# Retention and a mixture of experts on one core: a state read spread over four array quarters, empty rows written one per pass, fill branches on two engines

## The chip, the cores and the metric

The kernel runs on one core of one Trainium2 chip. Its five engines are TensorE (PE in the profile; PEld is its weight load), VectorE (DVE), ScalarE (ACT), GpSimd (POOL) and SyncE (SP); each takes its instructions from a queue of its own, in order. The metric is the time of one execution on the device in microseconds (us), as the median of several runs.

## The reference

Inputs are q, k and v of 4 sequences, 8 heads, 768 tokens and 64 columns, two gates of 512 x 8 and, for each of 8 experts, w1 (512 x 1024) and w2 (1024 x 512). Cut to what matters:

```python
for t in range(S):                       # attention: a decaying state for each head
    state = gamma * state + k[t] outer v[t]
    y[t] = scale * q[t] @ state
x = y as rows of tokens (3072 x 512)
e_idx = argmax(x @ w_gate); gate_w = probability of e_idx; eom = sigmoid(x @ w_output_gate)
for e in range(E):                       # each token goes to one expert
    out[mask] = gate_w * eom[e] * (relu(x[mask] @ w1[e]) @ w2[e])
```

## The kernel before, in words

**Attention.** A sequence has six chunks of 128 tokens, taken in pairs: `j` counts 12 pairs, `NJ` = 3 to a sequence, and `c` is the chunk in a pair. Eight heads stand in four groups `g` of two halves `hh` (partitions 0 to 63 and 64 to 127). For a pair, `scores` (L349) multiplies k and q of each chunk, and VectorE masks the result into `ams[c]` (L359). `inter` (L367) reads the state: a matmul of 64 rows by 64 columns for each head, from `sd[j, c]` into the PSUM banks `py[0]` and `py[1]`, one bank for a chunk. For the second chunk the halves of the output are exchanged (`half[hh ^ c]`), so that the two chunks' matmuls lie on all four 64 x 64 quarters of the array. In the first pair of a sequence (j % NJ == 0) the first chunk has no state to read and is skipped; the second chunk's matmuls then lie on two quarters. `attend` (L376) adds the masked scores times v, bank by bank; `weigh` (L384) multiplies a bank by the decay `gq` on VectorE and writes `yts`. `state` (L390) updates the state. `turn_k` (L324, L328) and `turn_q` (L342, L346) transpose the next pair's k and q on PE and copy them out. For the pair before, `logits` (L407), `route1`, `exps`, `gates`, `counts` and `places` find each token's expert and row, `tokens` (L508) transposes y back, `rows` (L515, L518) copies it scaled into `row` on ScalarE, one copy for the first chunk and two for the second, whose halves are exchanged, and `scatter` (L532) writes its rows by an indirect DMA of GpSimd into `srt`, a table in HBM sorted by expert with 448 slots to each. `prep_q` (L298) and `prep_v` (L290) rearrange q and scale v. Before j = 1, `more_gq` (L282) builds `gq` chunk by chunk.

**Branches.** Where an expert has few tokens, slots have to be filled with empty rows. `fill` (L543) does this on GpSimd and VectorE under a condition read into a register: `late` (L734) in iteration j = 10, behind `inter(10)`, and `n_low` (L831) behind the last attention work. The register is loaded, and the branch taken, on all five engines. In the profiled execution nothing is filled.

**Experts.** The expert with the most tokens after a third of the work is started early: `run_head` works off its first 224 slots as matmuls between the last attention steps (L622, L643). Then eight passes follow, each with eight stages `s` of 128 hidden columns: `stage1` (L899) is 12 matmuls into `h`, `relu` (L903, L904) splits it into two parts, and `stage2` (L917) of the stage two before is 12 matmuls into `a`. Pass 0 is the rest of the first expert, 224 slots wide; passes 1 to 7 are 436 to 364 wide, by the number of tokens. `load_x` (L853) loads a pass's rows from `srt`, a pass ahead; `turn_x` and `low_x` (L872 to L883) transpose and split them into `xh` and `xw`. `load_weights` (L142, L146) brings the weights, `split_weights` (L159 to L165) splits them on ScalarE and VectorE. `emit_head` and `emit` (`send`, L177) write finished rows to the output by indirect DMAs of GpSimd.

**Empty rows.** Slots of an expert from 320 up to its end that hold no token are written with empty rows by `pad` (L187), one indirect DMA for each expert. One is issued in `head_load`; `new_pad` issues the others: three behind ReLU steps of `run_head` (`hd["relu", 5]` to `hd["relu", 7]`), and four in pass 0, each behind a `stage2` (`done`). `load_x(e)` waits for write `e`. A write is declared independent of the row loads in `x0`, which holds those of pass 0 alone. On GpSimd's queue the writes of pass 0 stand among the outputs of `emit_head`.

Of the kernel before, what the change touches and what calls it, by code (L numbers as in the profile page):

```python
# [15 lines left out]
AF = mybir.ActivationFunctionType  # L16
ALU = mybir.AluOpType
# [9 lines left out]
SEG = 130  # L27
ROW = 4 * SEG
NOID = float(1 << 20)


@with_exitstack
def retention_moe_kernel(
# [14 lines left out]
    nc = tc.nc  # L48
    P = 128
# [152 lines left out]
    with tc.manual_schedule(engines=None), ExitStack() as actx:  # L202
# [76 lines left out]
                nc.gpsimd.tensor_copy(gqn[h, 1], gqn[half[1 - n], 0])  # L279

        def more_gq(c, engine):
            engine.tensor_tensor(out=gq[:, c], in0=gqn[:, c % 2].rearrange("p g (t r) -> p g r t", r=2),  # L282
                                 in1=gc[:, c % 2, c, :].unsqueeze(2).unsqueeze(3).broadcast_to([P, NG, 2, 64]), op=ALU.mult)

        def prep_v(j, engine, parts=1):
            c0, src = 2 * (j % NJ), vn.pop(j)
# [77 lines left out]
        def open_y():  # L364
            rt["py"] = [ps_1.tile([P, 512], F32, name="py", tag=f"y{c}") for c in range(2)]

        def inter(j):  # L367
            for g in range(NG):
                for c in range(2):
                    if j % NJ == 0 and c == 0:  # L370
                        continue
                    for hh in range(2):
                        nc.tensor.matmul(rt["py"][c][half[hh ^ c], g * P:(g + 1) * P], sd[j, c][half[hh], g],  # L373
                                         qt[j][half[hh], g, c], start=(g == 0), stop=False, skip_group_check=True)

        def attend(j, c):  # L376
            py = rt["py"][c]
            for g in range(NG):
                for hh in range(2):
                    mm = nc.tensor.matmul(py[half[hh ^ c], g * P:(g + 1) * P], vs[j][:, c, 2 * g + hh], ams[c][:, hh, g],  # L380
                                     start=(j % NJ == 0 and c == 0 and g == 0), stop=True, skip_group_check=True)
            return mm.ins

        def weigh(j, c):  # L384
            if c == 0:
                yts[j] = ap.tile([P, 2, NG, P], F32, name="yt", tag="yt", bufs=2)
            nc.vector.tensor_tensor(out=yts[j][:, c].rearrange("p g t -> p (g t)"), in0=rt["py"][c],
                                    in1=gq[:, 2 * (j % NJ) + c].rearrange("p g r t -> p (g r t)"), op=ALU.mult)

        def state(j, c):  # L390
            if j % NJ == 0 and c == 0:
# [10 lines left out]
        def logits(j):  # L402
            misc = rt["misc"] = ps_1.tile([P, 512], F32, name="misc", tag="misc" if j + 1 < NPR else "st")
            for i in range(2):
                for t in range(4):
                    c, g = t // 2, 2 * (t % 2) + i
                    nc.tensor.matmul(misc[32 * t:32 * t + 32, 0:P], wg[:, c, g], yts[j][:, c, g], start=(i == 0), stop=(i == 1),  # L407
                                     tile_position=(0, 32 * t))
            lt = sm.tile([P, P], F32, name="lt", tag="lt")
            nc.scalar.copy(lt, misc[:, 0:P])  # L410
            rt["lt"] = lt
# [99 lines left out]
        def rows(j):  # L511
            px = rt.pop(("px", j))
            gate = rt.pop(("g", j))
            row = rt["row", j]
            nc.scalar.activation(row[:, 0, :, 0:P].rearrange("p a (dc j) -> p dc a j", j=32),  # L515
                                 px[:, 0].rearrange("p (dc a j) -> p dc a j", a=4, j=32), AF.Copy, scale=gate[:, 0:1])
            for x in range(2):
                nc.scalar.activation(row[:, 1, 2 - 2 * x:4 - 2 * x, 0:P].rearrange("p a (dc j) -> p dc a j", j=32),  # L518
                                     px[:, 1].rearrange("p (dc x a j) -> p x dc a j", x=2, a=2, j=32)[:, x],
                                     AF.Copy, scale=gate[:, 1:2])  # L520

        def labels(j):
# [175 lines left out]
        prep_q(1, nc.vector)  # L698
        state(0, 0)
        attend(0, 0)  # L700
        weigh(0, 0)
        more_gq(1, nc.vector)
        inter(0)
        turn_q(1, True)
        state(0, 1)
        turn_k(1, True)
        attend(0, 1)
        weigh(0, 1)
        swap_gates()
        last_consts()  # L710
# [3 lines left out]
        for j in range(1, NPR - 1):  # L714
            if j + 2 < NPR:
                load_pair(j + 2)
            if j - 1 == PICK + 1:
                read_pick()
            if j in w_at:
                load_weights(w_at[j])  # L720
            if j - 2 == EARLY:
                scatter(j - 2, 0)
                scatter(j - 2, 1)
            prep_q(j + 1, nc.gpsimd, [rt["done"]] if j >= 2 else ())
            prep_v(j + 1, nc.gpsimd)
            if j >= 2 and j - 2 != EARLY:
                scatter(j - 2, 0)
            open_y()
            scores(j, (lambda: state(1, 0)) if j == 1 else None)
            if j - 1 in w_at:  # L730
                cast_weights(w_at[j - 1])
            inter(j)
            if j == EARLY + 2:
                n_late = nc.values_load(late[0:1, 0:1], min_val=0, max_val=1)  # L734
                with tc.If(n_late > 0):
                    fill(base0, cnt0, 0, HEAD, sm)
                head_load()
                load_weights(4)
            logits(j - 1)
            turn_k(j + 1)  # L740
            turn_l(j - 1)
            route1(j - 1)
            exps(j - 1)
            attend(j, 0)
            weigh(j, 0)
            if j % NJ < NJ - 1:
                state(j, 1)
            turn_q(j + 1)
            gates(j - 1)
            for c in {1: (3, 4), 2: (5,)}.get(j, ()):  # L750
                more_gq(c, nc.vector)
            if j - 1 in w_at:
                low_weights(w_at[j - 1])
            if j - 2 == PICK:
                choose()
            tokens(j - 1)
            labels(j - 1)
            rows(j - 1)
            counts(j - 1)
            if j >= 2 and j - 2 != EARLY:  # L760
                scatter(j - 2, 1)
            places(j - 1)
            if j - 1 == PICK:
                sort8(cnts, io8, pick)
            if j - 1 == EARLY:
                judge()
            attend(j, 1)
            weigh(j, 1)
            state(j + 1, 0)
# [58 lines left out]
        cast_weights(6)  # L828
        run_head(12)
        low_weights(6)  # L830
        n_few = nc.values_load(n_low[0:1, 0:1], min_val=0, max_val=E)  # L831
        with tc.If(n_few > 0):
            for e in range(E):
                fill(float(e * SLOTS), cnts[:, e:e + 1], FILL - P, FILL, sm)
            n_few = nc.values_load(n_low[0:1, 1:2], min_val=0, max_val=E)
            with tc.If(n_few > 0):
                for e in range(E):
                    fill(float(e * SLOTS), cnts[:, e:e + 1], 0, FILL - P, sm)

    with tc.manual_schedule(engines=None), ExitStack() as mctx:  # L840
# [7 lines left out]
        def load_x(e):  # L848
            r0, n = PASS[e]
            nb = math.ceil(n / 32)  # L850
            t = mp.tile([P, NB, SEG], F32, name="xl", tag="xl")
            for a in range(4):
                ld = nc.sync.dma_start(  # L853
                    t[32 * a:32 * a + 32, 0:nb],
                    srt[ds(r0, 32 * nb), a * SEG:(a + 1) * SEG].rearrange("(n i) x -> i n x", i=32))
                if e == 0:
                    behind(ld, sent)
                    x0.append(ld.ins)
                else:
                    behind(ld, pads[e:e + 1])  # L860
                    for o in pads[:e] + pads[e + 1:]:
                        tc.declare_no_dep(ld.ins, o, reason="other experts' rows")
            xr[e] = t

        def turn_x(e, dc):
# [103 lines left out]
            nc.vector.tensor_scalar(out=t, in0=m, scalar1=0.25, scalar2=None, op0=ALU.mult)  # L969
            return t  # L970

        x0 = []
        pads = list(hd["pad"])

        def new_pad(after):
            r = len(pads)
            o = pad(padr[:, r - 1:r])
            behind(o, [after])
            for ld in x0:
                tc.declare_no_dep(o.ins, ld, reason="other experts' rows")  # L980
            pads.append(o.ins)

# [24 lines left out]
        nc.vector.tensor_scalar(out=padr, in0=fj, scalar1=slot, scalar2=None, op0=ALU.add)  # L1007
        new_pad(hd["relu", 5])
        run_head(24)
        new_pad(hd["relu", 6])  # L1010
        run_head(12)
        turn_x(0, 0)
        turn_x(0, 1)
# [28 lines left out]
        for s in range(NS + 2):  # L1042
# [9 lines left out]
                relu = stage1(s)  # L1052
            if s >= 2:
                done = stage2(s - 2)
                if s - 2 < NF and len(pads) < E:
                    new_pad(done)
                if f == 1:
                    copy_out(s - 2)
            if e == 0:
# [9 lines left out]
                        split_weights(n)  # L1069
            if s == NS - NF + 3:  # L1070
                idl = prep_idl(idm)
            if e == 0:
                if f < HEAD // 32:
                    behind(emit_head(f), [relu])
            elif s < NS and f >= 1:
                for n in range(2 * f - 2, min(math.ceil(PASS[e - 1][1] / 32), 2 * f)):
                    behind(emit(e - 1, n), [done if n % 2 else relu])
# [130 lines left out]
```

## Time and profile before

| what | value |
|---|---|
| three timed runs, us | 430.78, 431.31 (median), 432.47 |
| the profiled execution, us | 432.42 |
| its span in the profile, us | 430.65 |
| PE busy | 413.7 us, 96% |
| VectorE, ScalarE, GpSimd busy | 264.4, 179.3, 190.2 us |
| DMA | 74.06 MB, mean 172 GB/s |

The span runs from the first instruction of the program to the last; the execution's own time has some 1.8 us more. A timeline or chain row reads: start and duration in us, engine, line, operation, output<-inputs, number of instructions merged, and in brackets the idle time of the engine ahead of it with what ended it. "issue" there stands for time in which the engine waited for nothing that the profile shows. A row of stretches reads: window, its length, then for each engine the busy time and the number of its instructions, the granted clock of TensorE as a share of full speed, the DMA engines' busy share and what they moved. Attention runs up to about 124 us, the head of the first expert up to 148 us, the passes up to 420 us.

### The profile page before, as it was taken

What the parts mean: (1) busy time and instruction counts of PE and PEld (TensorE: products, weight loads), DVE (VectorE), ACT (ScalarE), POOL (GpSimd) and SP (SyncE); (2) the same over time, 40 slices, a digit from 0 to 9 for tenths busy, and PEclk for the clock granted to TensorE, in tenths of its full rate; (3) what the DMA queues carried; (4) which work ended last, traced back from release to release, by engine and by line L of the source; (5) the groups of instructions that cost most, each with busy time, mean ns of one, the idle gap of its engine ahead of it and who ended that gap; (6) DMA issues with size and microseconds to landing.
All of it is one profiled execution on the core that took longest, in us unless ns stands there. A gap on an engine that the chain in (4) does not pass through costs nothing.

```text
span 430.7 us, 10299 instructions
## 1 busy us (share of the span) xinstructions
PE 413.7 (96%) x3700; PEld 392.0 (91%) x3700; DVE 264.4 (61%) x703; ACT 179.3 (42%) x395; POOL 190.2 (44%) x257
## 2 busy tenths in 40 slices
PE   8999999999999998999999999999999999999990
PEld 4888999999879997899999999999999999999990
DVE  2888778778778765766466556655646656754120
ACT  2244565646436233635335334443434443542120
POOL 6558666676624217060045426405515524523512
PEclk9999999999999999999999999999999999999995
DMA  9999999995562398494475395485558458420102
GB/s 192 208 225 255 258 268 248 275 269 176 144 223 102 74 250 272 146 270 153 135 172 173 122 198 171 137 188 167 177 151 206 137 176 197 159 59 19 44 7 74
DMA packets 126566, 74.06 MB, mean 172 GB/s; under 512 B 56686, under 2 KB 114930, under 8 KB 126504
## 3 DMA queue, kind: packets, MB, share of 16 engines
q1 hardware_dynamic: 119568, 59.30, 55.1%
q0 software_dynamic: 5728, 13.93, 9.3%
q8 instruction: 31, 0.51, 0.5%
q14 instruction: 31, 0.25, 0.2%
q10 hardware_dynamic: 1208, 0.06, 0.2%
HBM read 59.35 MB, written 15.23 MB: 173 GB/s over the span
## 4 chain that ended last, share of the span: by engine, by line
PE 80%; issue 9%; DMA 3%; POOL 3%; DVE 2%; SPq 1%; ACT 1%; POOLq 0%; DVEq 0%; ACTq 0%
PE h L899 26%; PE a L917 26%; PE w L356 5%; PE py L380 5%; PE py L373 3%; POOL out_dram L177 3%; PE w L324 3%; PE w L342 2%; PE w L508 2%; PE st L396 2%; PE misc L407 2%; PE h L622 2%; DMA kn<-in_k_dram 1%; DMA srt<-row,posi 1%; PE w L643 1%
## 5 line engine op out<-in xcount | busy, mean ns | idle before, releaser
L177 POOL DMA_INDIRECT out_dram<-ot,idi x84 | 91.0, 1083 | 147.2 <-ACT whi L160 79.0
L899 PE MATMUL h<-xh,whi 128*128 128x224 f32 (+7 forms) x256 | 85.6, 334 | 1.1 <-issue 1.1
L899 PE MATMUL h<-xw,whi 128*128 128x224 f32 (+7 forms) x256 | 85.9, 335 | 0.6 <-issue 0.4
L899 PE MATMUL h<-xh,wlo 128*128 128x224 f32 (+7 forms) x256 | 85.4, 334 | 0.9 <-issue 0.9
L917 PE MATMUL a<-hh,whi 128*128 128x224 f32 (+7 forms) x256 | 85.8, 335 | 0.4 <-issue 0.3
L917 PE MATMUL a<-hl,whi 128*128 128x224 f32 (+7 forms) x256 | 85.8, 335 | 0.1
L917 PE MATMUL a<-hh,wlo 128*128 128x224 f32 (+7 forms) x256 | 85.7, 335 | 0.0
L904 DVE SCALAR_TENSOR_TENSOR hl<-h,hh 128x224 fp32r<-128x224 f32 (+7 forms) x64 | 35.0, 548 | 61.9 <-ACT hh L903 54.0
L903 ACT ACTIVATE hh<-h 128x224 fp32r<-128x224 f32 (+7 forms) x64 | 31.0, 484 | 82.1 <-PE h L899 74.7
L164 DVE TENSOR_TENSOR wlo<-raw,whi 128x512 fp32r<-128x512 f32 x64 | 43.9, 686 | 29.3 <-ACT whi L159 25.7
L159 ACT CAST whi<-raw 128x512 fp32r<-128x512 f32 x64 | 39.6, 619 | 37.7 <-PE a L917 33.4
L899 PEld LDWEIGHTS h<-xw,whi 128*128 128x128 f32 x256 | 48.2, 188 | 2.4 <-issue 1.3
L899 PEld LDWEIGHTS h<-xh,whi 128*128 128x128 f32 x256 | 48.2, 188 | 2.0 <-issue 1.6
L917 PEld LDWEIGHTS a<-hh,whi 128*128 128x128 f32 x256 | 48.2, 188 | 1.3 <-issue 0.9
L899 PEld LDWEIGHTS h<-xh,wlo 128*128 128x128 f32 x256 | 48.2, 188 | 0.9 <-issue 0.5
L917 PEld LDWEIGHTS a<-hl,whi 128*128 128x128 f32 x256 | 48.2, 188 | 0.6 <-DVE hl L904 0.2
L917 PEld LDWEIGHTS a<-hh,wlo 128*128 128x128 f32 x256 | 48.2, 188 | 0.4
L165 DVE TENSOR_TENSOR wlo<-raw,whi 128x512 fp32r<-128x512 f32 x64 | 43.8, 685 | 0.0
L160 ACT CAST whi<-raw 128x512 fp32r<-128x512 f32 x64 | 39.6, 618 | 0.1
L877 ACT CAST xh<-xt 128x416 fp32r<-128x416 f32 (+3 forms) x32 | 16.3, 513 | 40.4 <-DVE xt L876 29.8
L359 DVE TENSOR_TENSOR am<-w,mask 128x1024 f32<-128x1024 f32 x24 | 28.4, 1219 | 5.9 <-PE w L356 4.5
L532 POOL DMA_INDIRECT srt<-row,posi x24 | 24.7, 1030 | 11.0 <-issue 2.9
(183 smaller groups left out, 606.0 us busy)
## 6 DMA issues: line engine op xcount, KB each, us to landing
raw<-in_moe_w_dram SPq DMA_DIRECT2D x128, 256.0 KB
qn<-in_q_dram SPq DMA_DIRECT2D x12, 512.0 KB
kn<-in_k_dram SPq DMA_DIRECT2D x24, 256.0 KB
vn<-in_v_dram SPq DMA_DIRECT2D x24, 256.0 KB
xl<-srt SPq DMA_DIRECT2D x12, 211.2 KB
xl<-srt SPq DMA_DIRECT2D x12, 195.0 KB
out_dram<-ot,idi POOLq DMA_INDIRECT x84
xl<-srt SPq DMA_DIRECT2D x8, 113.8 KB
```

Of the source, the lines that this page charges most:

```text
L159: nc.scalar.copy(hi[:, 0], raw[:, 0])
L160: nc.scalar.copy(perm(hi), r2)
L164: nc.vector.tensor_sub(lo[:, 0], raw[:, 0], hi[:, 0].bitcast(F32))
L165: nc.vector.tensor_sub(perm(lo), r2, perm(hi).bitcast(F32))
L177: st = nc.gpsimd.indirect_dma_start(out=dst, out_offset=bass.IndirectOffsetOnAxis(ap=idx, axis=0), in_=src, in_offset=None, bounds_check=n ...
L356: nc.tensor.matmul(w[:, hh, g * P:(g + 1) * P], kt[j][half[hh], c, g], qt[j][half[hh], g, c], start=True, stop=True)
L359: nc.vector.tensor_tensor(out=a.rearrange("p b g t -> p (b g) t"), in0=w.rearrange("p b (g t) -> p (b g) t", g=NG), in1=mask.rearrange("p ...
L532: st = nc.gpsimd.indirect_dma_start(out=srt, out_offset=bass.IndirectOffsetOnAxis(ap=posi[:, c:c + 1], axis=0), in_=row[:, c].rearrange("p ...
L899: nc.tensor.matmul(ps[:, 0:C], l[:, 0, w], r[:, dc, 0:C], start=(n == 0), stop=(n == 3 * NDC - 1))
L903: relu = nc.scalar.activation(hh, ps[:, 0:C], AF.Relu)
L904: nc.vector.scalar_tensor_tensor(out=hl, in0=ps[:, 0:C], scalar=0.0, in1=hh.bitcast(F32), op0=ALU.max, op1=ALU.subtract)
L917: mm = nc.tensor.matmul(accs[d][:, 0:C], l[:, 1, w], r, start=(f == 0 and n == 0), stop=(f == NF - 1 and n == 2))
```

## The change

In the first pair of a sequence, `place` gives each chunk and group a bank, a place in it and whether its halves are exchanged: each bank then holds two groups of either chunk, and the second chunk's groups 2 and 3 aren't exchanged. `inter` goes through the groups in the order 0, 2, 1, 3; `attend` and `weigh` take a bank at a time, so that both chunks' masked scores are needed for the first bank (for j = 0 `attend` stays by chunk, and `weigh(0, 0)` moves behind `attend(0, 1)`). `more_gq(1)`, the gates in `logits` and the copies in `rows` follow the places; `rows` has four copies instead of three in these pairs. The register loads and branches at L734, L831 and L835 are made for GpSimd and VectorE alone. `new_pad` behind `hd["relu", 6]` and the four in pass 0 go; one stands at the first stage of each of the passes 1 to 5, behind that stage's ReLU. The writes are declared independent of all passes' row loads.

```diff
 NOID = float(1 << 20)
+FILLERS = (mybir.EngineType.Pool, mybir.EngineType.DVE)
...
         def more_gq(c, engine):
-            engine.tensor_tensor(out=gq[:, c], in0=gqn[:, c % 2].rearrange("p g (t r) -> p g r t", r=2),
-                                 in1=gc[:, c % 2, c, :].unsqueeze(2).unsqueeze(3).broadcast_to([P, NG, 2, 64]), op=ALU.mult)
+            for g, x in ((slice(0, 2), 1), (slice(2, 4), 0)) if c == 1 else ((slice(0, NG), c % 2),):
+                engine.tensor_tensor(out=gq[:, c, g], in0=gqn[:, x, g].rearrange("p g (t r) -> p g r t", r=2),
+                                     in1=gc[:, x, c, g].unsqueeze(2).unsqueeze(3).broadcast_to([P, g.stop - g.start, 2, 64]),
+                                     op=ALU.mult)
...
+        def mixed(j):
+            return j % NJ == 0
+
+        def place(j, c, g):
+
+            if not mixed(j):
+                return c, g, c
+            return (c ^ g // 2, 2 * c + g % 2, c ^ c * (g // 2))
+
         def inter(j):
-            for g in range(NG):
-                for c in range(2):
-                    if j % NJ == 0 and c == 0:
-                        continue
-                    for hh in range(2):
-                        nc.tensor.matmul(rt["py"][c][half[hh ^ c], g * P:(g + 1) * P], sd[j, c][half[hh], g],
-                                         qt[j][half[hh], g, c], start=(g == 0), stop=False, skip_group_check=True)
-
-        def attend(j, c):
-            py = rt["py"][c]
-            for g in range(NG):
+            todo = [(g, c) for g in range(NG) for c in range(2)]
+            if mixed(j):
+                todo = [(g, 1) for g in (0, 2, 1, 3)]
+            for g, c in todo:
+                b, n, x = place(j, c, g)
                 for hh in range(2):
-                    mm = nc.tensor.matmul(py[half[hh ^ c], g * P:(g + 1) * P], vs[j][:, c, 2 * g + hh], ams[c][:, hh, g],
-                                     start=(j % NJ == 0 and c == 0 and g == 0), stop=True, skip_group_check=True)
+                    nc.tensor.matmul(rt["py"][b][half[hh ^ x], n * P:(n + 1) * P], sd[j, c][half[hh], g],
+                                     qt[j][half[hh], g, c], start=(j > 0 and g in ((0, 2) if mixed(j) else (0,))), stop=False,
+                                     skip_group_check=True)
+
+        def attend(j, i):
+            todo = [(c, g) for c in range(2) for g in range(NG) if (place(j, c, g)[0] if j and mixed(j) else c) == i]
+            for c, g in todo:
+                b, n, x = place(j, c, g)
+                for hh in range(2):
+                    mm = nc.tensor.matmul(rt["py"][b][half[hh ^ x], n * P:(n + 1) * P], vs[j][:, c, 2 * g + hh], ams[c][:, hh, g],
+                                          start=(j == 0 and c == 0 and g % 2 == 0), stop=True, skip_group_check=True)
             return mm.ins
...
-        def weigh(j, c):
-            if c == 0:
+        def weigh(j, i):
+            if i == 0:
                 yts[j] = ap.tile([P, 2, NG, P], F32, name="yt", tag="yt", bufs=2)
-            nc.vector.tensor_tensor(out=yts[j][:, c].rearrange("p g t -> p (g t)"), in0=rt["py"][c],
-                                    in1=gq[:, 2 * (j % NJ) + c].rearrange("p g r t -> p (g r t)"), op=ALU.mult)
+            c = 2 * (j % NJ)
+            out = yts[j].rearrange("p c (a g) t -> p (c a) (g t)", a=2)
+            by = gq[:, c:c + 2].rearrange("p c (a g) r t -> p (c a) (g r t)", a=2)
+            w = (slice(0, 4, 3) if i == 0 else slice(1, 3)) if mixed(j) else slice(2 * i, 2 * i + 2)
+            nc.vector.tensor_tensor(out=out[:, w], in0=rt["py"][i].rearrange("p (a x) -> p a x", a=2), in1=by[:, w], op=ALU.mult)
...
                     c, g = t // 2, 2 * (t % 2) + i
-                    nc.tensor.matmul(misc[32 * t:32 * t + 32, 0:P], wg[:, c, g], yts[j][:, c, g], start=(i == 0), stop=(i == 1),
+                    nc.tensor.matmul(misc[32 * t:32 * t + 32, 0:P], wg[:, place(j, c, g)[2], g], yts[j][:, c, g], start=(i == 0), stop=(i == 1),
                                      tile_position=(0, 32 * t))
...
                                  px[:, 0].rearrange("p (dc a j) -> p dc a j", a=4, j=32), AF.Copy, scale=gate[:, 0:1])
+            n = 2 if mixed(j) else NG
             for x in range(2):
-                nc.scalar.activation(row[:, 1, 2 - 2 * x:4 - 2 * x, 0:P].rearrange("p a (dc j) -> p dc a j", j=32),
-                                     px[:, 1].rearrange("p (dc x a j) -> p x dc a j", x=2, a=2, j=32)[:, x],
+                nc.scalar.activation(row[:, 1, 2 - 2 * x:4 - 2 * x, 0:P].rearrange("p a (dc j) -> p dc a j", j=32)[:, 0:n],
+                                     px[:, 1].rearrange("p (dc x a j) -> p x dc a j", x=2, a=2, j=32)[:, x, 0:n],
+                                     AF.Copy, scale=gate[:, 1:2])
+            if n < NG:
+                nc.scalar.activation(row[:, 1, :, 0:P].rearrange("p a (dc j) -> p dc a j", j=32)[:, n:],
+                                     px[:, 1].rearrange("p (dc a j) -> p dc a j", a=4, j=32)[:, n:],
                                      AF.Copy, scale=gate[:, 1:2])
...
         attend(0, 0)
-        weigh(0, 0)
         more_gq(1, nc.vector)
...
         attend(0, 1)
+        weigh(0, 0)
         weigh(0, 1)
...
             if j == EARLY + 2:
-                n_late = nc.values_load(late[0:1, 0:1], min_val=0, max_val=1)
+                n_late = nc.values_load(late[0:1, 0:1], engines=FILLERS, min_val=0, max_val=1)
                 with tc.If(n_late > 0):
...
         low_weights(6)
-        n_few = nc.values_load(n_low[0:1, 0:1], min_val=0, max_val=E)
+        n_few = nc.values_load(n_low[0:1, 0:1], engines=FILLERS, min_val=0, max_val=E)
         with tc.If(n_few > 0):
...
                 fill(float(e * SLOTS), cnts[:, e:e + 1], FILL - P, FILL, sm)
-            n_few = nc.values_load(n_low[0:1, 1:2], min_val=0, max_val=E)
+            n_few = nc.values_load(n_low[0:1, 1:2], engines=FILLERS, min_val=0, max_val=E)
             with tc.If(n_few > 0):
...
                     behind(ld, sent)
-                    x0.append(ld.ins)
                 else:
...
                         tc.declare_no_dep(ld.ins, o, reason="other experts' rows")
+                xloads.append(ld.ins)
             xr[e] = t
...
-        x0 = []
+        xloads = []
         pads = list(hd["pad"])
...
             behind(o, [after])
-            for ld in x0:
+            for ld in xloads:
                 tc.declare_no_dep(o.ins, ld, reason="other experts' rows")
...
         run_head(24)
-        new_pad(hd["relu", 6])
         run_head(12)
...
                 done = stage2(s - 2)
-                if s - 2 < NF and len(pads) < E:
-                    new_pad(done)
                 if f == 1:
...
                 idl = prep_idl(idm)
+            if e > 0 and f == 0 and len(pads) < E:
+                new_pad(relu)
             if e == 0:
```

## Rows read from the trace of the kernel before

**Rows 1.** The page, part 1: engine, busy us (share of the span), instructions.

```profile
PE 413.7 (96%) x3700; PEld 392.0 (91%) x3700; DVE 264.4 (61%) x703; ACT 179.3 (42%) x395; POOL 190.2 (44%) x257
```

**Rows 2.** Stretches: PE, PEld, DVE, ACT, POOL busy (instructions), clock, DMA share, GB/s.

```profile
38.60:48.30 9.70, 9.70 (x162) 8.87 (x161) 7.38 (x38) 5.36 (x15) 6.36 (x11) 1.00 1.07 276
...
136.00:140.00 4.00, 4.00 (x38) 4.00 (x37) 3.23 (x12) 2.78 (x6) 1.28 (x2) 1.00 0.35 135
...
152.00:168.00 16.00, 15.95 (x143) 15.76 (x142) 10.10 (x28) 7.03 (x15) 6.76 (x7) 1.00 1.06 283
168.00:176.00 8.00, 5.26 (x28) 3.98 (x28) 2.37 (x5) 1.65 (x4) 4.11 (x5) 1.00 0.28 104
...
200.00:379.00 179.00, 179.00 (x986) 178.02 (x985) 108.10 (x191) 76.24 (x145) 71.00 (x65) 1.00 0.60 166
```

**Rows 3.** The chain that ended last: `inter` of j = 1 and j = 3.

```profile
21.03 1.03 PE py L373 x32
...
40.59 1.02 PE py L373 x16
```

**Rows 4.** The timeline of j = 3: the masks and the first `attend`.

```profile
39.95 2.36 DVE L359 TENSOR_TENSOR am<-w,mask 128x1024 f32<-128x1024 f32 x2
...
43.24 0.99 PE L380 MATMUL py<-am,vs 128*64 128x128 f32 x14
```

**Rows 5.** The timeline of j = 0 and 1.

```profile
13.64 0.76 DVE L298 COPY qr<-qn 128x512 f32<-128x512 f32 x2
14.21 1.23 PE L342 MATMUL w<-ident,qr 128*128 128x128 f32 x8
14.31 0.69 DVE L387 TENSOR_TENSOR yt<-py,gq 128x512 f32<-128x512 f32 x1
...
23.80 0.23 DVE L422 TENSOR_REDUCE lg<-misc 128x32 f32<-128x64 f32 x1 [1.50 <-PE misc L415]
...
28.44 0.69 ACT L515 ACTIVATE row<-w,gate 128x512 f32<-128x512 f32 x1 [1.11 <-DVE gate L463]
...
29.03 0.82 ACT L518 ACTIVATE row<-w,gate 128x256 f32<-128x256 f32 x2
```

**Rows 6.** Line L518: count, ns min/median/max, first and last start; who waited (us, times).

```profile
L518 ACT ACTIVATE row<-w,gate x24: 463/477/487, 29.0 to 134.0; 128x256 f32<-128x256 f32 x24
...
  PEld w L356: 0.3, 1
```

**Rows 7.** Lines L734 and L831, PE's own register loads, columns as in rows 6.

```profile
L734 PEldq TENSOR_LOAD <-late x1: 486/486/486, 108.7 to 108.7; - x1
...
L831 PEldq TENSOR_LOAD <-n_low x1: 312/312/312, 137.9 to 137.9; - x1
```

**Rows 8.** The timeline of PE: `inter(10)`.

```profile
107.30 1.09 PE L373 MATMUL py<-qt,sd 64*64 64x128 f32 x25
...
109.44 0.42 PE L373 MATMUL py<-qt,sd 64*64 64x128 f32 x2 [0.30 <-issue]
```

**Rows 9.** The timeline of pass 0: pass 1's rows, empty rows, outputs.

```profile
161.15 0.18 DVE L872 CAST idi<-xl 128x14 int32<-128x14 f32 x1 [1.38 <-DMA xl<-srt]
...
161.98 0.98 POOL L187 DMA_INDIRECT srt<-zrow,padr  x1 [7.67 <-PE h L899]
...
172.35 0.98 POOL L177 DMA_INDIRECT out_dram<-ot,idx  x1 [0.30 <-issue]
```

**Rows 10.** The chain at the end of pass 0: groups of 12 matmuls.

```profile
166.98 1.34 PE a L917 x12
...
176.07 2.37 PE h L899 x12
```

**Rows 11.** The timeline of the same stretch.

```profile
169.80 0.63 DVE L883 TENSOR_TENSOR xw<-xt,xh 128x448 fp32r<-128x448 f32 x1 [0.63 <-issue]
...
171.95 0.19 PEld L899 LDWEIGHTS h<-xh,whi 128*128 128x128 f32 x1 [0.84 <-issue]
...
174.92 0.36 ACT L903 ACTIVATE hh<-h 128x224 fp32r<-128x224 f32 x1 [5.15 <-PE h L899]
```

## Prediction before the result was known

> **What bounds the kernel now.** I read the page first: its busy shares name the engine that is hardly ever idle, TensorE (PE), with 413.7 us of a span of 430.7 [rows 1]. The table of stretches comes next, because a share over the whole span hides stages. PE has no idle time in an attention iteration (9.70 of 9.70 us) and none from 200 to 379 us (179.00 of 179.00), with the granted clock full; but from 168 to 176 us it works 5.26 us of 8.00 [rows 2]. So there are two ways to shorten this kernel: give PE less to do, or close that hole. The timeline and the chain then show what each edit touches. The profiled execution took 432.42 us (span 430.65, 1.77 us around it); the median of the three timed runs is 431.31. I make the sum against 432.42 and carry the difference, 1.11 us, over to the median.
>
> **The state read on four quarters.** In the first pair of each sequence (j = 0, 3, 6, 9) `inter` has only the second chunk to read, and all its matmuls use two of the four 64 x 64 quarters. Its 16 records take 1.02 us; in the other pairs 32 records on four quarters take 1.03 us [rows 3]. So 16 records on four quarters should need 0.51 us, and 0.51 us is saved per first pair. In j = 3, 6 and 9 PE waits for nothing, so I count 3 x 0.51 = 1.53 us. What could now be late: `attend(j, 0)` newly needs the masked scores of both chunks. In j = 3 VectorE finishes the second mask at 39.95 + 2.36 = 42.31 and `attend` starts at 43.24, so after a gain of 0.51 there are 0.42 us left [rows 4]. Were that cover gone, the cost would be the shortfall, at most 0.51 per pair. The weighing keeps one instruction per bank; that it now writes two pieces I cost at nothing, since VectorE waits 1.50 us for PE behind the masks [rows 5].
>
> In j = 0 I count no gain. The group behind `inter`, `turn_q(1)`, starts at 14.21 and reads `qr`, which VectorE finishes at 13.64 + 0.76 = 14.40, half of it earlier; PE would come sooner and wait [rows 5]. The moved `weigh(0, 0)`, 0.69 us, and the split `more_gq(1)` push the masks of j = 1 back by about 0.7 us; that lies under the 1.50 us that VectorE waits at 23.80 [rows 5]. Moreover PE is held 0.3 us, once, by the row copies of j = 0 [rows 6], and the change makes their two copies of 256 elements into two of 128 and one of 256. The copy of 512 elements takes 0.59 us from start to start (28.44 to 29.03), the two of 256 together 0.82, the second alone 0.48 [rows 5, 6]; by a slope of 0.24 us per 256 elements a copy of 128 takes some 0.23 us, so the three take 0.23 + 0.23 + 0.48 = 0.94, and PE's wait grows by about 0.1 us. After j = 3, 6 and 9 it is hidden: the one wait is all that PE has for them [rows 6]. Sum for this part: -1.53 + 0.1 = -1.43 us; bounds +0.1 (no overlap at all) and -2.0 (j = 0 gains as well).
>
> **Branches on GpSimd and VectorE alone.** PE, ScalarE and SyncE lose a register load and a branch at two places. PE's own loads take 0.49 us at 108.7 and 0.31 at 137.9 [rows 7]. At the second place PE is busy 4.00 of 4.00 us, so its queue covers them [rows 2]. At the first there is a gap of 0.30 us, but inside `inter`'s own matmuls, which stand ahead of the branch in the program [rows 8]. I take 0; the bounds are 0 and -0.5 (the first load uncovered). SyncE's next work, loads of sorted rows, is put behind GpSimd's scatters in any case; VectorE and GpSimd keep their branches. The Trainium skill, page "Runtime: NRT & Kernel Launch", section "Instruction fetch mechanics", says that a taken branch can force a fetch of code before execution goes on. By that rule the gaps at 108 us would go with the branch; by the row of stretches for the second place nothing is lost at one. The first reading is the third rival below.
>
> **Empty rows, one write per pass.** Of eight such writes, four stand in pass 0 and four ahead of it; afterwards three stand ahead and one at the first stage of each of passes 1 to 5. In pass 0 the first of the four starts at 161.98 after GpSimd idled 7.67 us. The releaser that the row names, a PE group, had long finished; what had just landed is the load of pass 1's rows, for which VectorE waited until 161.15 [rows 9]. The new kernel frees these writes from all row loads. From 161.98 to 172.35 + 0.98 = 173.33 GpSimd runs nine indirect DMAs end to end, the four writes and five outputs held up behind them, while the DMA engines are busy at 1.06 of their capacity up to 168 us [rows 2, 9]. Meanwhile PE stumbles. A 224-wide group takes 1.34 us and a 436-wide one 2.37; the group of 166.98 ends at 168.32, so behind one group of each width the next should begin at 172.03, and it begins at 176.07, 4.0 us late, in gaps (0.84 us the longest) for which the trace names no wait [rows 10, 11]. ScalarE waits 5.15 us, until 174.92, for a group that PE had ended at 166.98 [rows 10, 11]: what PE has done reaches others late. The trace doesn't say why. The smaller stumble at 108 us has the same look, and it too stands beside row writes that GpSimd sends one after the other. So I take the run of nine as the cause, and the hole as gone with it. Next late is the last quarter of pass 1's rows, ready at 169.80 + 0.63 = 170.43 [rows 11]; PE, ten matmuls of twelve into the group of 168.32, would ask for it at about 170.3, so 0.1 us comes back. Net -3.9 us; bounds 0 (the weight loads alone did it) and -4.0. The five later writes take GpSimd 0.98 us each [rows 9]. At a pass's first stage its queue holds no output, so nobody waits behind them, and each stands a pass ahead of the load that needs it: 0 us.
>
> **Sum.** -1.43 + 0 - 3.9 = -5.3 us: 427.1 for an execution like the profiled one, 426.0 as a median.
>
> **Rivals.**
> 1. The hole stays, because the weight loads of pass 0 cause it and not the writes. For: the DMA engines were full from 152 us on [rows 2]. Against: PE ran on under that load, 15.95 of 16.00 us, until the nine came [rows 2]. Time: 431.31 - 1.43 = 429.9.
> 2. The hole half closes: the outputs still run through full DMA engines, but no longer end to end. -1.43 - 1.9: 428.0.
> 3. The branch owned the gaps at 108 us as well: there `inter` took from 107.30 to 109.86 instead of 1.03 us, 1.5 us more [rows 3, 8]. With the hole closed: 426.0 - 1.5 = 424.5. Against it is the covered branch at 138 us.
> 4. Slower: each write brings its stumble along into its new pass. Four writes went with 4.0 us, 1.0 each; if the hole stays for the weights' sake and five writes at the heads of passes 1 to 5 cost 1.0 us each, the time is 431.31 - 1.43 + 5.0 = 434.9. It turns into slower by over 0.5% from (1.43 + 2.16) / 5 = 0.72 us per write. For: PE has no slack there at all. Against: GpSimd runs 65 operations between 200 and 379 us and PE never gaps [rows 2].
> 5. The matmuls don't overlap on four quarters in this order: then only the hole counts, 431.31 - 3.9 + 0.1 = 427.5. Against it are the groups of 32 records.
>
> **How the numbers follow.** About 0.5% (2.16 us) is what a measurement of this kernel can tell from no change. Chances: forecast 0.40, first rival 0.25, second 0.14, third 0.07, fourth 0.08, fifth 0.06. The predicted time is the forecast's, 426.0. The range reaches from 424.5, the third rival, to 430.4, the first with half a microsecond of spread; beyond lies mainly the fourth. Faster: forecast, second, third and fifth, 0.67, less 0.02 for a hole that closes by less than half: 0.65. Same: 0.25 + 0.02 = 0.27. Slower: 0.08.
>
> **What would show it.** `inter` of j = 3, 6 and 9 with 16 records in 0.5 us, each such iteration 0.5 us shorter, and j = 0 unchanged. No idle time of 7 us on GpSimd ahead of an empty-row write in pass 0, and the first expert's outputs spaced by stage, some 2.7 us apart. PE busy nearly throughout between 168 and 176 us, ScalarE's wait of 5 us gone. PE without gaps in the passes that now hold the five writes. The gaps at 108 us stay if the branch is innocent. The prediction falls if the hole is there again without the run of nine, or if new gaps stand beside the writes at the heads of passes.

## The result and the profile after

Beside the kernel before (431.7 us, median of four runs, 430.78 to 432.47), the changed kernel takes 426.11 us (four runs, 425.29 to 426.66): ratio 0.9866, 95% interval 0.9832 to 0.9900, 5.6 us less. The profiled execution took 426.66 us, its span is 424.9. First its page's busy times, as in [rows 1]:

```profile
PE 410.5 (97%) x3700; PEld 390.9 (92%) x3700; DVE 263.0 (62%) x704; ACT 180.1 (42%) x399; POOL 189.9 (45%) x257
```

PE is busy for 3.2 us less with the same 3700 instructions. Where the time went is seen in the stretches of its trace, with the columns of [rows 2] (window and length; PE, PEld, DVE, ACT, POOL; clock, DMA share, GB/s): the iteration of j = 3, that of j = 10, most of pass 0, the eight microseconds in which the hole of before would lie, and the later passes.

```profile
38.57:47.86 9.29, 9.29 (x161) 8.46 (x161) 7.02 (x32) 4.70 (x14) 6.42 (x11) 1.00 1.03 261
104.08:114.87 10.79, 10.23 (x174) 9.07 (x174) 8.20 (x35) 6.12 (x16) 7.96 (x12) 1.00 0.41 129
151.43:166.60 15.17, 15.17 (x134) 15.15 (x135) 9.26 (x19) 6.46 (x14) 5.97 (x6) 1.00 1.04 281
166.60:174.60 8.00, 7.80 (x50) 7.15 (x49) 7.37 (x15) 6.20 (x13) 1.19 (x1) 1.00 0.34 107
199.00:378.00 179.00, 179.00 (x991) 178.27 (x990) 107.79 (x190) 76.01 (x144) 75.57 (x69) 1.00 0.60 168
```

PE's 5.26 of 8.00 us in [rows 2] has become 7.80 of 8.00: the hole is gone. The five writes now lie in the later passes (69 GpSimd operations instead of 65 in nearly the same window) and PE is busy there throughout, so none of them costs anything. The chain of waits dates the gains (start, duration, engine, group; the groups shown are the scores of j = 3, 4, 10 and 11, and the groups at the start and the end of pass 0):

```profile
38.57 1.99 PE w L359 x32
47.86 1.99 PE w L359 x32
...
104.08 1.99 PE w L359 x32
...
114.87 1.99 PE w L359 x32
...
151.43 1.49 PE a L940 x11
...
169.25 1.34 PE a L940 x12
170.58 2.37 PE h L922 x12
```

In the chain of before the same groups begin at 38.60, 48.32, 105.39, 116.50, 153.43 and, for the last, 176.07 [rows 10]. So 1.31 us are gained up to j = 10, 0.32 in that iteration, 0.37 up to 151.43, and 3.49 between there and the end of pass 0 (22.64 us before, 19.15 after). The spans differ by 5.75 us; the remaining 0.26 come behind it.

The two places at which the change touches PE's order, in the timeline of after: `inter` of j = 3 with the group behind it, and `inter` of j = 10 where the branch used to be.

```profile
40.48 0.67 PE L386 MATMUL py<-qt,sd 64*64 64x128 f32 x16
41.08 0.64 PE L425 MATMUL misc<-yt,wg 128*32 128x128 f32 x16
...
107.36 0.47 PE L386 MATMUL py<-qt,sd 64*64 64x128 f32 x4 [0.26 <-issue]
108.13 0.67 PE L425 MATMUL misc<-yt,wg 128*32 128x128 f32 x16 [0.30 <-issue]
```

From start to start the read takes 0.60 us instead of 1.02 [rows 3]. The gaps near 108 us are still there without a branch on PE.

### The profile page after: what moved, and what is told of

Read it like the earlier page. It is cut to its first block, busy times and chain, and to the rows that moved or that the text cites. A ratio compares the mean times of both kernels' runs of the same rounds, so it can differ in the third digit from the quotient of the medians.

```text
span 424.9 us, 10288 instructions
## 1 busy us (share of the span) xinstructions
PE 410.5 (97%) x3700; PEld 390.9 (92%) x3700; DVE 263.0 (62%) x704; ACT 180.1 (42%) x399; POOL 189.9 (45%) x257
## 4 chain that ended last, share of the span: by engine, by line
PE 80%; issue 9%; DVE 5%; POOL 3%; ACT 2%; POOLq 0%; DVEq 0%; ACTq 0%
PE h L922 25%; PE a L940 24%; PE w L359 5%; PE py L395 5%; POOL out_dram L178 3%; PE w L327 3%; PE w L345 3%; PE h L645 3%; PE py L386 3%; PE w L526 2%; PE st L414 2%; PE misc L425 2%; PE w L666 2%; PE w L314 1%; DVE xt L899 1%
```

## The experiments

The theory with which I went in: 1.3 us from the quarters, nothing from the branches, 3.5 us from the run of nine GpSimd transfers that the moved and freed writes break up. The rivals: the writes' number rather than their run, the branch, or the mere shift of pass 0 against its weight loads. The runs came in four sets, each on a chip of its own, and each kernel was timed against the kernel before on the same chip.

| set | kernel | median, us | before there, us | ratio (95% interval) |
|---|---|---|---|---|
| 1 | quarters | 423.12 | 424.85 | 0.9963 (0.9949 to 0.9976) |
| 1 | branch | 423.86 | 424.85 | 0.9975 (0.9962 to 0.9988) |
| 1 | writes | 424.83 | 424.85 | 1.0003 (0.9984 to 1.0022) |
| 1 | free | 424.58 | 424.85 | 0.9991 (0.9976 to 1.0006) |
| 2 | again_after | 422.71 | 424.94 | 0.9952 (0.9935 to 0.9969) |
| 2 | turn | 423.00 | 424.94 | 0.9958 (0.9943 to 0.9974) |
| 3 | order | 422.82 | 424.34 | 0.9966 (0.9953 to 0.9980) |
| 3 | branch2 | 424.35 | 424.34 | 0.9993 (0.9980 to 1.0006) |
| 3 | writes2 | 424.61 | 424.34 | 1.0003 (0.9990 to 1.0016) |
| 4 | writes3 | 424.92 | 424.30 | 1.0010 (0.9991 to 1.0029) |

Two more were profiled and timed once: again_before (423.18 us, set 2) and run14 (423.65 us, set 3). The column to look at first is the fourth: the kernel before takes 424.3 to 424.9 us in all four sets, 7 us less than beside the changed kernel. The second thing is that the whole change is worth 0.5% there and not 1.3%.

**One part at a time: quarters, branch, writes (set 1).** Each is the kernel before with one hunk of the change: quarters has all that stands in `more_gq` to `rows` and the moved `weigh(0, 0)`; the other two are these lines:

```diff
branch, branch2 (at L734, L831 and L835)
+            n_late = nc.values_load(late[0:1, 0:1], engines=FILLERS, min_val=0, max_val=1)
...
writes, writes2, writes3
-        new_pad(hd["relu", 6])
...
-                if s - 2 < NF and len(pads) < E:
-                    new_pad(done)
...
+            if e > 0 and f == 0 and len(pads) < E:
+                new_pad(relu)
...
-                    x0.append(ld.ins)
+                xloads.append(ld.ins)
```

> The kernel before with the four-quarter state read alone: branches and empty rows as they were. My theory: inter of j = 3, 6 and 9 takes 0.6 us (measured so in the changed kernel) instead of 1.02, so 3 x 0.42 = 1.3 us at most are gained up to j = 10, and some 0.3 us more as the changed kernel shows between j = 10 and the head; the hole at the end of pass 0 stands as it did. That gives 431.7 - 1.3 = 430.4 us, ratio 0.997. Rival: the hole has nothing to do with the writes but with when pass 0 comes relative to its weight loads; then a start that is 1.3 us earlier changes it, and the hole is smaller or larger by over 1 us.

> The kernel before with the branches on GpSimd and VectorE alone. My theory: nothing on the path; the gaps at 108 us stay, 431.7 us within 0.4, ratio 0.999 to 1.000. Rival: the branch owns some of the gaps at 108 us (three steps of some 0.7 us before, two in the changed kernel) and some of the 0.35 us that the changed kernel gains between 122 and 151 us; then inter(10) takes at least 0.7 us less than in the kernel before, and the time is 430.6 to 431.0.

> The kernel before with the empty rows alone moved to one per pass and freed of the row loads. My theory: the hole at the end of pass 0 closes but for some 0.5 us that PE waits for the last quarter of pass 1's rows; from 153.4 to 176.1 us the kernel before needs 22.6 us and the changed one 19.15, so 3.5 us are gained: 428.2 us, ratio 0.992. Rival: the hole closes only because the start of pass 0 has moved along with the first part of the change; then it stays here, at 431.5 to 432.

The quarters come out as expected, 0.0037 x 424.85 = 1.6 us (1.0 to 2.2), and 1.26 us of it are seen in the trace, 0.42 per read. (In the iteration of j = 3 of that one trace the 0.42 us are spent again on a wait for row copies of ScalarE, 0.22 us of idle time at 39.45: 9.78 us from scores to scores, against 9.71 in again_before; at j = 6 and 9 they are kept.) The writes give nothing where 3.5 us were expected. The branch seemed to give 1.06 us, more than its bound.

**free.** The writes keep their places in pass 0 and lose only their ties to the row loads:

```diff
-                    x0.append(ld.ins)
                 else:
...
+                xloads.append(ld.ins)
             xr[e] = t
```

> The kernel before, with the four writes of empty rows left in pass 0 at their places in the program, but freed of every row load, so that they run when GpSimd reaches them. My theory (a run of indirect DMAs that follow one another while the DMA engines are full makes PE stumble): four writes and five outputs are then spread over the pass, no nine in a run, and the hole is gone: 428.2 to 428.7 us. Rival (the four extra writes in pass 0 add too much traffic beside the weight loads, in whatever order): the hole stays with at least 2.5 us of its 4, wherever in the pass it falls: 430.5 or more.

Neither theory's number is met: 424.58 us, the same as before there. There was nothing to close in set 1, so it decides nothing between them. Nor did the edit break up the run: in its trace the four writes and five outputs still follow one another, from 151.57 us on, all but the last of them 0.30 to 0.33 us apart. They run earlier, beside DMA engines at 1.20 (150 to 154 us) and 1.11 (154 to 158), and PE is busy 4.00 of 4.00 us in both stretches.

**again_before, again_after (set 2).** Both kernels unchanged, to see the kernel before without its hole.

> The kernel before, unchanged, profiled once more on the chip of this set of runs, since it took 424.85 us in the first set of experiments and 431.7 us beside the changed kernel. Theory A (the hole at 168 us and the smaller stumbles at 108, 120 and 149 us belong to the chip or the session, not to the run of nine alone): here a span near 423 us shows PE busy 8.00 of 8.00 us at the end of pass 0, with the nine GpSimd transfers still end to end. Theory B (the run of nine always makes the hole, and the parts tried so far each broke it by a chance shift): the hole is in this trace, 3 us or more, at whatever total.

> The whole change, timed against the kernel before on this set's chip. If the stumbles of PE are absent here as in the first set: quarters alone gave 1.6 us, the branches alone 1.0, the writes 0.0, so 424.85 - 2.6 = 422.2 us, ratio 0.994. If they are present (before near 431.7): 426.1, ratio 0.987, as in the first measurement. If the gains of the two parts overlap (both move the same stage): 423.1, ratio 0.996.

The stretches of again_before, columns as above; the first four lie where the trace of [rows 2] and [rows 8] stumbles, the last two in the run of nine:

```profile
107.00:110.00 3.00, 2.94 (x63) 2.33 (x55) 2.01 (x4) 0.67 (x2) 2.74 (x4) 1.00 0.50 186
119.00:122.00 3.00, 3.00 (x37) 2.49 (x34) 3.00 (x9) 2.18 (x4) 0.77 (x1) 1.00 0.90 255
148.00:150.00 2.00, 2.00 (x18) 1.88 (x17) 1.77 (x11) 0.71 (x2) 1.69 (x2) 1.00 0.90 263
168.00:176.00 8.00, 8.00 (x47) 7.68 (x46) 6.78 (x14) 4.01 (x8) 1.93 (x2) 1.00 0.89 242
156.00:160.00 4.00, 4.00 (x38) 4.00 (x38) 2.83 (x6) 2.05 (x4) 2.94 (x3) 1.00 1.11 342
160.00:164.00 4.00, 4.00 (x38) 4.00 (x38) 2.74 (x6) 1.39 (x3) 3.03 (x4) 1.00 0.93 328
```

The same windows in the first trace of the kernel before; PE misses 0.60, 0.55 and 0.25 us there, and 2.74 us in the hole of [rows 2]:

```profile
107.00:110.00 3.00, 2.40 (x48) 1.63 (x48) 1.73 (x3) 0.81 (x2) 2.69 (x5) 1.00 0.50 193
119.00:122.00 3.00, 2.45 (x50) 1.53 (x44) 2.25 (x6) 0.67 (x3) 1.11 (x2) 1.00 0.98 304
148.00:150.00 2.00, 1.75 (x12) 1.33 (x11) 1.76 (x7) 0.76 (x2) 0.42 (x1) 1.00 0.18 70
```

And what GpSimd does in again_before meanwhile, the first three, the sixth and the last of the run:

```profile
156.45 0.98 POOL L187 DMA_INDIRECT srt<-zrow,padr  x1 [6.22 <-PE a L917]
157.74 0.98 POOL L177 DMA_INDIRECT out_dram<-ot,idx  x1 [0.30 <-issue]
159.03 1.05 POOL L187 DMA_INDIRECT srt<-zrow,padr  x1 [0.30 <-PE a L917]
...
162.96 0.98 POOL L177 DMA_INDIRECT out_dram<-ot,idx  x1 [0.30 <-DMA srt<-zrow,padr]
...
166.83 1.15 POOL L177 DMA_INDIRECT out_dram<-ot,idx  x1 [0.30 <-ACT whi L159]
```

That is the pattern of [rows 9] again: an idle stretch that ends 0.83 us behind VectorE's first work on pass 1's rows (155.62 there, 161.15 in [rows 9]), then four writes and five outputs end to end, 0.30 us apart, for the first 4 us beside DMA engines as full (1.11) as in [rows 2]. PE does not lose a tenth of a microsecond. So theory B falls: the run of nine does not make the hole by itself, nor do the weight loads. again_after gives 0.0048 x 424.94 = 2.0 us (1.3 to 2.8), as much as the quarters alone within the intervals.

**run14 (set 3).** A stronger dose: all outputs of a pass in one run.

```diff
-                for n in range(2 * f - 2, min(math.ceil(PASS[e - 1][1] / 32), 2 * f)):
-                    behind(emit(e - 1, n), [done if n % 2 else relu])
+                for n in range(math.ceil(PASS[e - 1][1] / 32)) if f == 3 else ():
+                    behind(emit(e - 1, n), [relu])
```

> The changed kernel with all outputs of a finished pass, up to 14, sent by GpSimd in one run at the fourth stage of the next pass, instead of two per stage. If a run of GpSimd transfers makes PE stumble by itself, PE loses time in each pass from 200 to 378 us (now 178.00 of 178.00 us busy), up to 14/9 x 4 = 6 us a pass. If the hole belonged to the chip of the first measurement: no idle time of PE, except that the last output lands no later; the same time as the changed kernel within 1 us.

One stretch of it, from the first to the last of the fourteen outputs of pass 1:

```profile
216.60:234.60 18.00, 18.00 (x97) 17.86 (x97) 11.61 (x21) 8.40 (x16) 13.90 (x14) 1.00 0.52 164
```

Fourteen transfers in 18 us and PE busy 18.00 of 18.00: no idle time, as the second theory expected. The DMA engines are at 0.52 here, so this speaks for a long run alone; the full engines are in again_before.

**branch2, writes2, writes3 (sets 3 and 4).** Repeated for two reasons: the branch's 1.06 us, and the chance of a chip on which PE stumbles.

> The same kernel as in the run named branch, on this set's chip. There it came out at 0.9975 (0.9962 to 0.9988), 1.06 us, although its PE work ended at 412.10 us, between 411.92 and 412.45 of the two kernels that keep the old branches. If the gain is real: 0.9975 again. If it was a property of that set: 1.000 within 0.0013.

> The same kernel as in the run named writes (the kernel before with the empty rows alone moved and freed), on this set's chip. If PE stumbles on this chip as in the first measurement (before near 431.7): the hole closes, 3.5 us are gained, ratio 0.992, and the smaller stumbles at 108 and 120 us stay. If it does not (before near 424.9, as on the two chips since): nothing, ratio 1.000.

> The kernel with the empty rows alone moved and freed, once more, on whatever chip this set is given. Where PE stumbles (before near 431.7, as beside the changed kernel): the hole at 168 us is gone, ratio 0.992, and the stumbles at 108 and 120 us stay, which would make the run of nine the trigger on such a chip. Where it does not (before near 424.5, as on the three chips so far): 1.000 within 0.002, and what sets the first measurement apart stays open.

The branch gives 0.9993, 0.3 us (from 0.3 lost to 0.8 gained), so the 1.06 us of the first reading do not stand. What the branch costs PE can be read where it stands: `inter(10)` and the group behind it, in the timelines of writes, with PE's branch between the two, and of branch, without it.

```profile
107.18 1.10 PE L373 MATMUL py<-qt,sd 64*64 64x128 f32 x32
108.34 0.65 PE L407 MATMUL misc<-yt,wg 128*32 128x128 f32 x16
...
107.17 1.10 PE L374 MATMUL py<-qt,sd 64*64 64x128 f32 x32
108.21 0.64 PE L408 MATMUL misc<-yt,wg 128*32 128x128 f32 x16
```

From start to start this is 1.16 us with the branch and 1.04 without. The twelve traces of the four sets fall into two groups here: 1.16 to 1.21 us in the six with PE's branch (again_before, quarters, writes, free, writes2, writes3), 1.03 or 1.04 in the six without it (branch, branch2, again_after, order, run14, turn). So this branch costs PE 0.13 us. At the second one nothing shows: around 138 us the head's groups of 12 stand 1.34 us apart in writes and in branch. At the end of the program 0.13 us is lost in other differences: PE's last group starts at 410.35 us in branch, and at 410.17 and 410.70 in free and writes. From there to the end of their spans (421.6, 421.9, 423.1) it is 11.3, 11.7 and 12.4 us: part of what separates such executions comes behind PE's work. The writes give 1.000 twice more; no set met the 431.7 us again.

**order (set 3).** The prediction's fifth rival, tried on the order of the matmuls:

```diff
-                todo = [(g, 1) for g in (0, 2, 1, 3)]
+                todo = [(g, 1) for g in range(NG)]
```

> The changed kernel with the 16 matmuls of a sequence's second chunk issued by head group 0, 1, 2, 3 instead of 0, 2, 1, 3. Groups 0 and 1 (and 2 and 3) lie in the same bank and the same pair of quarters, so neighbours then share quarters two by two. Theory (the overlap depends on neighbours lying on different quarters): each of the three reads takes 0.8 us or more instead of 0.60, 0.6 us lost in all. Rival (the matmuls find their quarter within a few instructions, whatever the order): 0.60 us as before, 0.0 lost.

`inter` of j = 3 in its timeline, with the group behind it:

```profile
40.19 0.68 PE L386 MATMUL py<-qt,sd 64*64 64x128 f32 x16
40.80 0.64 PE L425 MATMUL misc<-yt,wg 128*32 128x128 f32 x16
```

0.61 us against 0.60: between these two orders of the groups there is no difference; what the change gains is that all four quarters are used.

**turn (set 2).** An attempt on the wait that the change leaves at the end of pass 0:

```diff
-                for dc in {4: (0,), 5: (1,), 6: (2, 3)}.get(f, ()):
+                for dc in {4: (0,), 5: (1,)}.get(f, ()):
                     prep_x(1, dc)
+                if f == 6:
+                    turn_x(1, 2)
+                    turn_x(1, 3)
+                    low_x(1, 2)
+                    low_x(1, 3)
```

> The changed kernel, with the last two quarters of pass 1's rows turned one behind the other on VectorE (transpose, transpose, subtract, subtract) instead of each after its own cast. In the changed kernel's trace VectorE idles 0.63 us between transpose and subtract, and PE waits 0.64 us in all for those rows at 167.9 and 168.6. My theory: where PE does wait there, 0.6 us are gained; where PE comes later than the rows (PE waited for nothing there in the experiments with the first two parts alone), 0.0. Rival: the subtract of the third quarter, now 0.6 us later, is what PE asks for next, and nothing is gained in either case.

423.00 against 422.71 us, the same within the intervals. On that chip PE waits for these rows in neither kernel, so the case in which it could pay did not come up.

## Why the prediction was right, and where it was not

**The sum.** 426.0 us forecast, 426.11 measured. In the profiled executions 5.3 us were forecast and 5.75 came. That the sum fits so closely is in part luck: the quarters gave 0.12 us less than forecast and the end of pass 0 0.41 less, and 0.95 us came in at places that the prediction had at nothing (0.32, 0.37 and 0.26, above).

**The quarters.** Forecast 1.43 us, found 1.31 at j = 10. The mis-sized term is the read itself: I took it as half of a read of 32 records, 0.51 us, and it takes 0.60, so a pair saves 0.42 and three save 1.26. The 0.1 us from the row copies of j = 0 came as said (the half of the scores that they hold up begins at 30.03 instead of 29.90 us) but was made up again by j = 3, 38.57 against 38.60. That j = 0 gains nothing holds too: the timeline has `turn_q(1)` waiting 0.47 us for `qr`. The cover of 0.42 us ahead of `attend` was enough: the masks end at 42.39, `attend` starts at 42.78 (timeline of after).

```profile
14.31 1.23 PE L345 MATMUL w<-ident,qr 128*128 128x128 f32 x8 [0.47 <-DVE qr L301]
...
40.03 2.36 DVE L362 TENSOR_TENSOR am<-w,mask 128x1024 f32<-128x1024 f32 x2 [0.56 <-PE w L359]
...
42.78 0.98 PE L395 MATMUL py<-am,vs 128*64 128x128 f32 x14
```

Beside the branch's 0.13 us below, this is the only part of the gain that the other sets show. From the scores of j = 4 to those of j = 10, with two such reads between, the first measurement has 57.07 us before and 56.22 after; in the sets each trace with the old read has 57.1 there and each with the new one 56.2.

**The branches.** Forecast 0, with 0.5 us as the bound; found 0.13 us at the first branch and nothing at the second, which PE's queue covers as said. The first was put at nothing because the gap at 108 us stands ahead of the branch in the program; that does not show the branch to be covered. The rival by which they owned the gaps at 108 us falls twice: the gaps stand in after without a branch, and they are all but absent in again_before with it (2.94 of 3.00 us). The rule of the Trainium skill, page "Runtime: NRT & Kernel Launch", section "Instruction fetch mechanics", may be behind the 0.13 us; whether the register load, the branch or a fetch takes them, no run here tells apart.

**The empty rows.** Forecast 3.9 us, and 3.49 went. The step about what comes late next was too small: 0.1 us was forecast, and PE waits 0.17 us at 167.91 and 0.47 us at 168.57 for the last quarters of pass 1's rows, 0.64 in all. Of the other signs, three came as described: no idle stretch of 7 us ahead of a write in pass 0, ScalarE's wait of 5.15 us [rows 11] gone, no gap beside the later writes. The first expert's outputs are not spaced evenly by some 2.7 us; they start 1.3 to 4.1 us apart.

But the cause that I gave is not upheld. "So I take the run of nine as the cause" was argued from one trace, in which the run and the hole stand side by side, and I had written that the trace doesn't say why. again_before has the same run beside equally full engines and no hole, and moving or freeing the writes gave nothing that can be measured in three sets. At most the run triggers something that only the first measurement had. What the first measurement had could not be tried, since no set came upon it again. Two things set its traces apart. PE stumbles in the trace of before at four places and not at one, each beside or just behind indirect transfers of GpSimd, and in after as well (10.23 of 10.79 us at j = 10). And the list of transfers, from issue to landing, has no landing times, first that of before (tensors, queue, operation, count, KB each, and, where there is one, the median us to landing):

```profile
raw<-in_moe_w_dram SPq DMA_DIRECT2D x128, 256.0 KB
```

and the same line of again_before:

```profile
raw<-in_moe_w_dram SPq DMA_DIRECT2D x128, 256.0 KB, 3.7
```

Counted over the traces, before has 4196 landing records and after 4346, against 5650 in again_before and 5662 in again_after. Since the trace's waits are named from such records, a gap without a named wait may here be a wait whose record is missing. Whether the chip (that of the first measurement is not on record), the occasion or the recording makes PE stumble stays open; so does whether it was the broken-up run that closed the hole there. For it: four executions of before had taken 430.78 to 432.47 us and four of after 425.29 to 426.66, and in pass 0 the writes are what changed. Against a firm word: pass 0 also began 2.0 us earlier.

**The rivals.** The weight loads alone (first rival) are out as a sufficient cause, for the same reason as the nine. The second, a hole half closed, does not fit: 3.49 of 4.0 us went. The slower case fell with PE's 179.00 of 179.00 us. The fifth fell with the 0.60 us, in either order. What I should have listed and did not: that the hole belongs to the measurement. Then the change is worth its quarters and the 0.13 us of the branch, 1.4 us together; measured were 1.6 us (quarters), 2.0 (again_after) and 1.4 (order, 0.0034 x 424.34) in three sets, all within the 0.5% that I had called the limit of what can be told.

**The rest.** 0.32 us at j = 10 and 0.37 between 115 and 151 us were not forecast. Of the first, 0.13 is the branch. The others lie at the stumbles (`inter(10)` lost two steps instead of three, and PE's idle time from 119 to 122 us is 0.30 us in after instead of 0.55); why they were smaller is open.

## What to carry to other kernels

A gap for which the trace names no wait is a poor thing to base a sum on: it may belong to the execution. Profile the same kernel a second time, on another chip, before counting on its removal. Work taken off an engine that waits for nothing, like the quarters' 0.42 us a read, keeps its gain from chip to chip. When a smaller part seems to gain more than its bound, repeat it before explaining it, and read it where it acts: the branch's 0.13 us show between two groups of PE, in twelve traces, where the times of whole executions can't tell them from nothing.

## What the hardware showed that I had not expected

One kernel took 431.7 us in one measurement and 424.3 to 424.9 us in four others, with the granted clock at 0.99 in both of its traces; of the 9.2 us between the two profiled spans (430.65 and 421.4) 4.1 us show as idle time of PE in the four windows above. By the starts of the same groups in the two chains, the stretches that hold these windows take 7.5 us longer: 1.32 in the iteration of j = 10 (11.11 against 9.79), 0.98 from there to the head, 1.15 in the head up to pass 0 and 4.05 in pass 0. So idle time shows only part of a stumble. GpSimd's indirect transfers, nine end to end beside DMA engines at 1.11 or fourteen at 0.52, took nothing from PE elsewhere. A register load and a branch on PE cost it 0.13 us behind `inter(10)` and nothing in the head. And 16 matmuls of 64 x 64 on four quarters take 0.60 us where 32 take 1.03: halving the number does not halve the time.
